# Clustered attention with a Fourier-gated second stage, one core: the order of all engines' work planned anew

## The chip, the cores and the metric

One core of a Trainium2 chip runs the kernel alone. The metric is the time of one execution in device microseconds; the kernel before took 384.34 us in the median of three runs (382.85 to 384.55). The profile is that of one further execution.

## The reference

```python
q_n = q / (norm(q) + 1e-06); k_n = ...; c_n = ...          # q, k, v: (4, 8, 768, 64), 16 centroids a head
q_assign = argmax(einsum('bhsd,hcd->bhsc', q_n, c_n)); k_assign = ...
mask = q_assign[:, :, :, None] == k_assign[:, :, None, :]
scores = where(mask, (q @ k.T) / 8, -1e9)
attn_out = softmax(scores) @ v                              # then heads side by side: x (4, 768, 512)
x1, x2, x3 = split(x @ w_proj, 3)                           # 512 -> 3 * 512
x2_conv = irfft(rfft(x2) * rfft(filter_fft))                # along the 768 positions
out = (x1 * x2_conv * x3) @ w_out
```

The first half is attention in which a query sees only the keys that were assigned to its own centroid. The second half takes the result through three projections, a circular convolution along the sequence (done as products with cosine and sine tables), a gate and an output projection.

## The kernel before, in words

**Attention.** Batches and heads are cut into 8 groups of four heads (`n`), each of two head pairs (`pr`): 16 head pairs. For a group, `routing` transposes q and k on TensorE (L583, L594), copies them out of PSUM (L586, L596, into tile qkP), casts them into the bf16 operands `aug` (L600, the helper's lines 265 for ScalarE and 267 for VectorE and POOL), multiplies with the centroids (L614) and turns the argmax into mask rows, which a DMA adds to the operands (L488). `attention` goes over six key blocks (`sk`) of a pair. For each it forms three score products of 512 columns (helper `product`, L75 as two 64-column halves or L73 as one 128-column product; 288 in all), three exponentials on ScalarE (L697, L700) and eight matmuls with v (L711), which need all three. VectorE sums the exponentials into `acc` (L728 for the first two blocks, in thirds that POOL may also do; L732 for the other four). At a pair's end ScalarE copies the output out of PSUM (L735, osb). The denominators are summed over partitions, either on TensorE (L745, then `total`, L751 and L753, tile den), or for middle groups by accumulating DMAs of POOL (L765), a trip through DRAM (dd, dp) and a small sum on VectorE (`gather`, L775 and L776). Then come a reciprocal (L778), a trip through DRAM that spreads it (dr, then rb by two SP transfers, L782), and one multiplication that gives xT (L811).

**Second stage.** `hyena` runs once a batch (two groups): projections `U` (L845) with copies and sums in tiles tm and uv2 (L854, L859, L864), the spectrum (L466, L872) and its products with the filter (L875, L879, tile y), gate projections `G` (through L75) with copies into x3 (L913, tile x) and products (L916), inverse transforms `I` with copies into od (L939), sums and folds (L941, L951), the gate (L954), and the output projection `W` with copies into ob (L974) and stores (L981). For the first three batches it runs beside the attention of later groups; for the last one it is the kernel's end.

**What sets the order.** `build` makes 1938 pieces. Each has a priority (its due time, in the planner's own clock), the engines that may do it with an assumed duration each, what it reads and writes, and the PSUM bank it opens or frees. `Plan.place` (L114) walks through assumed time: it takes for each engine the pieces that could start, prefers the smallest due time, and so fixes the engine and the place in the engine's queue. `NUDGE` (L41) adds a number to each piece's due time and `ONLY` (L42) fixes the engine of a few hundred pieces. The engines then run their queues strictly in that order, each instruction waiting on semaphores for its inputs. Assumed times are used for nothing else. Banks are handed out by `banks_for` (L223): at most four banks are in use for scores and four for the other work, and a product waits until the bank's earlier reader has ended.

**The shared port.** Pieces marked `lock=True` are SBUF work on VectorE or POOL that the planner keeps from overlapping. In the program, each such POOL piece waits for the last locked VectorE piece placed ahead of it (L1193); VectorE does not wait for POOL. Before the change `gather` has the mark `kind="port"`: it does hold POOL in the program (L1196), but the planner does not know of it.

Of the kernel before, what the change touches and what calls it, by code (L numbers as in the profile page):

```python
# [35 lines left out]
LEAD = 2.99901  # L36
FIRST = 2
BUSY = 8.09741
# [39 lines left out]
class Plan:  # L78
# [6 lines left out]
    def op(self, eng, fn, due, r=(), w=(), alloc=None, free=(), lock=False, byts=0, after=(), kind=None, lat=0.0):  # L85
# [27 lines left out]

    def place(self, free0, banks_for, switch=0.1, wait=0.1, rate=215e3, bonus=10.84378, margin=0.02195, shape=1.63806):  # L114
        free = dict(free0)
        bank_free = [0.0] * 8
        ready = {e: [] for e in free}
        pend = 0
        st = SimpleNamespace(pool=0.0, dve=0.0, bw={}, last=None, kind=None, score=0, o=0, tail=0,
                             held=dict(score=0, fill=0, o=0))  # L120
        st.scores, st.otiles = (sum(o.alloc is not None and o.alloc.cls == c for o in self.ops) for c in ("score", "o"))
        busy = dict.fromkeys(free, 0.0)

        def enqueue(o):
            o.ready = max([d.end - AFTER.get(d.on, 0.0) * (d in o.soft) + (0.06 if o.eng.keys().isdisjoint((d.on,)) or d.byts else 0.0)
                           for d in o.deps] or [0.0])
            if o.kind == "load":
                o.ready = max(o.ready, o.due - LEAD)
            for e in o.eng:
                ready[e].append(o)  # L130

        def take(o):
            if o.alloc is None:
                return
            o.alloc.ids = banks_for(o.alloc, bank_free, st, o)[0]
            for i in o.alloc.ids:
                bank_free[i] = 1e9
            st.score += o.alloc.cls == "score"
            st.o += o.alloc.cls == "o"
            st.held[HOLD.get(o.alloc.cls, "fill")] += o.alloc.n  # L140
            if o.alloc.cls != "o":
                st.tail |= st.o == st.otiles and any(i in (4, 5) for i in o.alloc.ids)

        def done(o, e, t, d, end):
            o.start, o.on = t, e
            o.end = end + AFTER.get(e, 0.0)
            if o.byts:
                s, b = max(o.end + 1.3, st.bw.get(e, 0.0)), o.byts / rate
                for f in [f for f in st.bw if f != e and st.bw[f] > s]:
                    b += min(o.byts / rate, st.bw[f] - s)  # L150
                    st.bw[f] += min(o.byts / rate, st.bw[f] - s)
                st.bw[e] = s + b
                o.end = st.bw[e] + 0.6 + o.lat
            if e == "POOL" and o.lock:
                st.pool = t + d
            if e == "DVE" and o.lock:
                st.dve = t + d
            for h in o.free:
                h.readers -= 1
                h.end = max(h.end, o.end)  # L160
                if not h.readers:
                    st.held[HOLD.get(h.cls, "fill")] -= h.n
# [12 lines left out]
        for o in self.ops:  # L175
            if not o.left:
                enqueue(o)
        while any(ready.values()):
            best = None
            for e, lst in ready.items():  # L180
                f = free[e]
                cand = []
                for o in lst:
                    t = max(f, o.ready)
                    m = margin if e == "PE" else 0.0
                    late = max(f, o.ready + m)
                    if o.alloc is not None:
                        ids = banks_for(o.alloc, bank_free, st, o)
                        if ids is None:
                            continue  # L190
                        t, late = max(t, ids[1]), max(late, ids[1] + m)
                    if o.lock and e in ("POOL", "DVE"):
                        t = late = max(t, st.dve if e == "POOL" else st.pool)
                    cand.append((late, o, t))
                if not cand:
                    continue
                t0 = min(c[0] for c in cand)
                c = min((c for c in cand if c[0] <= t0 + wait + 1e-9), key=lambda c: (
                    c[1].due - (bonus if e == "PE" and st.kind == "pv" == c[1].kind else 0.0)
                    + (shape if e == "PE" and array(c[1], st.last) != st.last else 0.0)  # L200
                    + (BUSY if e == "DVE" and len(c[1].eng) > 1 else 0.0)
                    + (c[0] - t0) * 20, c[1].seq))
# [45 lines left out]
def build(T):  # L248

    P = Plan()  # L250
    op = P.op
# [414 lines left out]
    def attention(n, pr, sins):  # L666
# [88 lines left out]
        if not last:  # L755
            if late:
                op(("SP", .6), lambda e: T.nc.sync.dma_start(T.dd[os][:4, :384], den_()[0:128:32]), te + 2, r=dk,
                   w=[("dd", os)], byts=6e3)
                op(("SP", .6), lambda e: T.nc.sync.dma_start(T.dn, T.dd[os][:4, :384].rearrange("z (a b) -> z a b", b=12)),
                   te + 4, r=[("dd", os)], w=["dn"], byts=6e3)  # L760
            else:
                flat_ = lambda: T.acc[os][:].rearrange("p a b -> p (a b)")
                rows = 64
                while rows >= ROWS:
                    op(("POOL", .8), lambda e, rows=rows: T.nc.gpsimd.dma_start(  # L765
                        flat_()[:rows], flat_()[rows:2 * rows], accum_op=Alu.add), te, r=[], w=AK,
                       byts=rows * 9e3, lat=1.5)
# [348 lines left out]
def kernel(  # L1116
# [70 lines left out]
    for o in order:  # L1187
# [40 lines left out]
```

## Time and profile before

| | |
|---|---|
| median of three runs | 384.34 us (382.85 to 384.55) |
| the profiled execution | 384.85 us, of which the span from first to last instruction is 383.1 |
| TensorE (PE) busy | 364.8 us |
| VectorE (DVE) busy | 347.5 us |
| ScalarE (ACT) busy | 261.6 us |
| POOL busy | 108.6 us |
| first product on TensorE | 4.67 us after the span's start |
| last head pair's last product with v | ends at 336.9 us |
| last matmul | near 378.5 us |

The page counts an engine as busy while an instruction of its own runs; the share of the span says how close it is to being the limit. "Waits" lines give, for an instruction, how long its engine stood idle before it and which instruction or transfer ended that. "The chain that ended last" is followed back from the last instruction, and each engine's share of it says whose work the end waited for. In timeline lines the columns are start in us, duration in us, engine, line, operation, output<-input, form, count, and in brackets the idle time before it with its releaser.

### The profile page before, as it was taken

The numbers are of one execution on the slowest core, as the hardware profiler recorded it, in microseconds if no ns is written. First come the engines' busy times: TensorE is split into PE (matmuls) and PEld (weight loads), VectorE is DVE, ScalarE is ACT, GpSimd is POOL, SyncE is SP. The second block draws the span as 40 slices with busy tenths as digits, with TensorE's granted clock in tenths as the row PEclk, the third lists the DMA queues.
The fourth block names the chain that finished last, engine by engine and source line by source line (L and its number), as shares of the span: only waits on it lengthen the run. The fifth ranks groups of instructions, "written<-read, shape, count | busy, mean of one in ns | idle before, by whom it ended". The sixth has DMA issues, their size and how long they took to land.

```text
span 383.1 us, 8652 instructions
## 1 busy us (share of the span) xinstructions
PE 364.8 (95%) x3323; PEld 208.3 (54%) x3328; DVE 347.5 (91%) x519; ACT 261.6 (68%) x488; POOL 108.6 (28%) x147
## 2 busy tenths in 40 slices
PE   2999998999999999999999999999999999999895
PEld 1564454445445565655555565656554565567682
DVE  8878997999899999989998999989999999899992
ACT  5996979787883978858856569688863747623332
POOL 8432101100022544123432453133320442103600
PEclk9999999999999999999999999999999999999999
DMA  9719965762578587747796876855555642110214
GB/s 221 160 47 220 164 154 135 158 146 63 128 165 157 104 130 151 126 90 122 160 144 147 165 191 134 173 72 89 103 75 132 134 105 37 46 43 2 94 74 164
DMA packets 93861, 47.19 MB, mean 123 GB/s; under 512 B 82088, under 2 KB 87676, under 8 KB 93820
## 3 DMA queue, kind: packets, MB, share of 16 engines
q1 hardware_dynamic: 88620, 37.03, 39.9%
q0 software_dynamic: 2704, 8.98, 17.6%
q10 hardware_dynamic: 2496, 0.62, 0.7%
q8 instruction: 26, 0.43, 0.5%
q14 instruction: 15, 0.12, 0.1%
HBM read 31.59 MB, written 7.40 MB: 102 GB/s over the span
## 4 chain that ended last, share of the span: by engine, by line
PE 55%; DVE 22%; DMA 9%; ACT 7%; issue 5%; SPq 1%; POOL 0%; POOLq 0%; DVEq 0%; ACTq 0%
PE bank L75 22%; PE pair L711 18%; DVE acc L732 5%; DMA rb<-dr 5%; PE bank L845 4%; ACT p L700 3%; DVE tm L875 2%; PE bank L583 2%; PE bank L594 2%; PE bank L614 1%; DVE acc L728 1%; DMA dr<-dn 1%; ACT p L697 1%; DVE xT L811 1%; PE bank L503 1%
## 5 line engine op out<-in xcount | busy, mean ns | idle before, releaser
L711 PE MATMUL pair<-p,vraw 128*64 128x385 f32 x768 | 142.5, 490 | 0.9 <-ACT osb L735 0.6
L700 ACT ACTIVATE p<-bank 128x512 f32<-128x512 f32 x192 | 108.9, 604 | 31.9 <-PE bank L75 26.5
L732 DVE TENSOR_TENSOR acc<-p,acc 128x1536 f32<-128x1536 f32 x64 | 113.0, 1765 | 4.9 <-ACT p L697 2.3
L711 PEld LDWEIGHTS pair<-p,vraw 128*64 128x64 f32 x768 | 53.7, 136 | 49.6 <-issue 42.5
L75 PE MATMUL bank<-aug,aug 80*64 80x512 bf16 (+3 forms) x688 | 75.2, 327 | 2.2 <-DVE den L753 0.5
L697 ACT ACTIVATE p<-bank 128x512 f32<-128x512 f32 x96 | 57.2, 606 | 11.6 <-PE bank L75 10.8
L75 PEld LDWEIGHTS <-aug 128*64 128x64 bf16 (+1 forms) x688 | 40.5, 109 | 38.9 <-issue 28.6
L765 POOL DMA_DIRECT2D acc<-acc x30 | 23.8, 793 | 91.1 <-DMA acc<-acc 42.6
L75 PE MATMUL bank<-xT,wpj 128*64 128x384 bf16 x488 | 44.7, 326 | 0.0
L267 POOL CAST aug<-qkP 64x768 bf16<-64x768 f32 x22 | 20.3, 927 | 71.7 <-DVE acc L732 34.1
L265 ACT COPY qkP<-bank 128x512 f32<-128x512 f32 (+1 forms) x52 | 26.7, 543 | 15.9 <-PE bank L75 8.6
L75 PEld LDWEIGHTS <-wpj 128*64 128x64 bf16 x488 | 29.6, 110 | 13.9 <-issue 3.8
L75 PEld LDWEIGHTS <-y 128*64 128x64 bf16 x512 | 25.5, 110 | 14.4 <-issue 4.4
L728 POOL TENSOR_TENSOR acc<-p,p 128x512 f32<-128x512 f32 x13 | 16.5, 1275 | 53.2 <-ACT p L700 25.7
L875 DVE TENSOR_TENSOR tm<-bank,hm 128x512 f32<-128x512 f32 x44 | 27.9, 681 | 1.0 <-POOL y L879 0.2
L728 DVE TENSOR_TENSOR acc<-p,p 128x512 f32<-128x512 f32 x35 | 24.6, 730 | 2.7 <-ACT p L697 1.7
L265 ACT CAST aug<-qkP 64x768 bf16<-64x768 f32 x29 | 24.0, 831 | 1.6 <-PE bank L75 1.1
L879 POOL TENSOR_TENSOR y<-tm 128x512 bf16<-128x512 f32 x17 | 21.7, 1289 | 10.5 <-DVE tm L875 6.3
L845 PE MATMUL bank<-wpj,xT 128*64 128x512 bf16 x192 | 22.7, 380 | 0.9 <-DVE xT L811 0.9
L75 PE MATMUL bank<-wout,y 128*64 128x512 bf16 x192 | 22.9, 379 | 0.0
L735 ACT COPY osb<-pair 128x770 f32<-128x770 f32 x16 | 12.9, 808 | 9.6 <-PE pair L711 9.5
L811 DVE SCALAR_TENSOR_TENSOR xT<-osb,rb 128x768 bf16<-128x768 f32 x15 | 15.2, 1012 | 3.9 <-DMA rb<-dr 3.9
(161 smaller groups left out, 440.7 us busy)
## 6 DMA issues: line engine op xcount, KB each, us to landing
qkraw<-in_k_dram SPq DMA_DIRECT2D x32, 192.0 KB, 4.6
vraw<-in_v_dram SPq DMA_DIRECT2D x16, 384.0 KB, 4.3
rb<-dr SPq DMA_DIRECT2D x30, 192.0 KB, 3.3
out_dram<-ob SPq DMA_DIRECT2D x11, 512.0 KB, 2.8
qkraw<-in_q_dram SPq DMA_DIRECT2D x29, 192.0 KB, 3.9
acc<-acc POOLq DMA_DIRECT2D x10, 384.0 KB, 4.9
acc<-acc POOLq DMA_DIRECT2D x10, 192.0 KB, 4.1
y<-in_moe_filter_fft_dram SPq DMA_DIRECT2D x4, 384.0 KB, 8.9
```

Of the source, the lines that this page charges most:

```text
L75: T.nc.tensor.matmul(out[64 * i:64 * i + 64], lhsT[:, 64 * i:64 * i + 64], rhs, start=start, stop=stop)
L265: T.nc.scalar.copy(out, in_)
L267: (T.nc.vector if e == "DVE" else T.nc.gpsimd).tensor_copy(out, in_)
L697: T.nc.scalar.activation(o, ap(h).rearrange("p (a b) -> p a b", a=2), Act.Exp, scale=0.125)
L700: T.nc.scalar.activation(flat(s)[:, lo:lo + 512], ap(h), Act.Exp, scale=0.125)
L711: T.nc.tensor.matmul(o[64 * hp:64 * hp + 64, ch, :385], T.vraw[vs][:, hp, sk * D:(sk + 1) * D], T.p[slots[sk]][:, hp, 384 * ch:384 * ch + ...
L728: alu(e).tensor_tensor(o, x, y, op=Alu.add)
L732: T.nc.vector.tensor_tensor(T.acc[os], T.p[slots[sk]][:, :, :S], T.acc[os], op=Alu.add)
L765: op(("POOL", .8), lambda e, rows=rows: T.nc.gpsimd.dma_start(flat_()[:rows], flat_()[rows:2 * rows], accum_op=Alu.add), te, r=[], w=AK, b ...
L845: T.nc.tensor.matmul(ap(h)[64 * i:64 * i + 64], T.xT[xs][:, kt, c:c + 64], T.wpj[:, kt, DM:2 * DM], start=kt == 0, stop=kt == ND - 1)
L875: op(("DVE", .68), lambda e, i=i, cs=cs, r=r, h=h: T.nc.vector.tensor_tensor(T.tm[r][:, cs], ap(h), hmrow(i, (0, 2, 2, 3)[2 * r + cs]), op ...
L879: op({"POOL": 1.5, "DVE": .68}, lambda e, i=i, r=r: alu(e).tensor_tensor(T.y[:, i, r], T.tm[r][:, 0], T.tm[r][:, 1], op=Alu.add if r else ...
```

## The change

Every due-time correction (`NUDGE`, now for all 1938 pieces instead of 1861) and the list of fixed engines (`ONLY`, 233 pieces instead of 227) are new. Four constants that entered the choice are set to zero (`LEAD`, `BUSY`, `bonus`, `shape`), and a piece that could start earlier is preferred less strongly (0.2 instead of 20 for each unit of assumed time). A locked POOL piece is planned to start 0.06 us after the locked VectorE piece instead of at its end, and the latest start that the choice compares keeps its margin. `gather` becomes a locked piece for the planner, and the mark "port" goes. The numbers of the new tables were sought with assumed durations that were scattered at random; the kernel holds only what was found. The pieces themselves, their sizes and their data are the same.

```diff
-LEAD = 2.99901
+LEAD = 0.0
...
-BUSY = 8.09741
+BUSY = 0.0
...
-NUDGE = {0:-51.9627,1:-2.6349,2:38.686,3:-141.578,4:142.779,5:166.407,
...
+NUDGE = {0:-27.3856,1:10.1217,2:73.8109,3:10.6856,4:400.544,5:336.601,
...
-ONLY = {25:"SP",26:"SP",27:"ACT",28:"ACT",29:"SP",30:"SP",53:"ACT",55:"ACT",56:"DVE",
...
+ONLY = {23:"SP",24:"SP",25:"SP",30:"SP",55:"ACT",56:"POOL",59:"ACT",62:"POOL",63:"DVE",
...
-    def place(..., bonus=10.84378, margin=0.02195, shape=1.63806):
+    def place(..., bonus=0.0, margin=0.02195, shape=0.0):
...
                     if o.lock and e in ("POOL", "DVE"):
-                        t = late = max(t, st.dve if e == "POOL" else st.pool)
+                        t = max(t, st.dve + 0.06 if e == "POOL" else st.pool)
+                        late = max(late, t)
...
-                    + (c[0] - t0) * 20, c[1].seq))
+                    + (c[0] - t0) * 0.2, c[1].seq))
...
-                op(("DVE", .68), gather, te + 6, r=["dp"], w=["dn"], kind="port")
+                op(("DVE", .68), gather, te + 6, r=["dp"], w=["dn"], lock=True)
...
-        elif o.on == "DVE" and (o.lock or o.kind == "port"):
+        elif o.lock and o.on == "DVE":
```

What this does to the engines, read from the two programs' instructions: 77 pieces that compute change their engine. Of the casts into `aug` (L600) 35 change among ScalarE, VectorE and POOL; of the first pair sums (L728) three go to POOL and five to VectorE; of the folds (L951) four go to POOL and three to VectorE; three copies into tm (L854), two into x (L913), two into od (L939) go from VectorE to ScalarE; copies of qkP, sim, ob, inv, fw and den go both ways. Each engine keeps nearly the order it had: a piece moves on average by 1.4 places on TensorE, 1.4 on ScalarE, 1.3 on VectorE, 0.7 on POOL and 0.85 on SP. At the start, the loads of the first q and k halves are dealt to SP's and ScalarE's queues in another way, and two more pieces of the angle tables (L359, L362) stand ahead of the centroids' normalisation (L325) on VectorE.

More of the change, by code (lines that the diff above doesn't have):

```diff
@@ new lines @@
+ONLY = {23:"SP",24:"SP",25:"SP",30:"SP",55:"ACT",56:"POOL",59:"ACT",62:"POOL",63:"DVE",75:"ACT",76:"ACT",81:"ACT",83:"DVE",84:"DVE",85:"DVE",87:"ACT",89:"DVE",123:"ACT",125:"DVE",131:"DVE",132:"DVE",134:"DVE",143:"ACT",145:"ACT",149:"ACT",151:"ACT",157:"ACT",161:"ACT",163:"ACT",178:"DVE",179:"DVE",228:"ACT",229:"DVE",235:"POOL",240:"POOL",241:"ACT",246:"POOL",247:"ACT",249:"ACT",250:"DVE",292:"DVE",357:"DVE",358:"POOL",359:"DVE",394:"DVE",404:"ACT",405:"ACT",407:"DVE",409:"DVE",410:"POOL",412:"DVE",416:"ACT",417:"ACT",420:"ACT",462:"POOL",464:"DVE",509:"ACT",514:"ACT",523:"DVE",525:"DVE",526:"DVE",533:"POOL",541:"POOL",549:"DVE",556:"ACT",560:"ACT",563:"DVE",567:"ACT",575:"ACT",578:"POOL",579:"POOL",580:"DVE",582:"ACT",595:"DVE",597:"ACT",601:"ACT",605:"ACT",609:"DVE",610:"DVE",612:"ACT",619:"ACT",624:"ACT",640:"DVE",641:"DVE",690:"ACT",691:"ACT",692:"POOL",693:"ACT",694:"POOL",695:"POOL",697:"DVE",699:"DVE",700:"ACT",701:"ACT",703:"POOL",705:"DVE",747:"DVE",810:"DVE",859:"ACT",860:"ACT",861:"ACT",863:"POOL",864:"ACT",866:"ACT",868:"ACT",871:"DVE",872:"ACT",874:"ACT",916:"POOL",917:"DVE",918:"DVE",965:"DVE",975:"ACT",989:"DVE",990:"POOL",997:"DVE",998:"POOL",1006:"DVE",1008:"ACT",1019:"POOL",1020:"POOL",1021:"DVE",1023:"ACT",1027:"ACT",1035:"DVE",1036:"POOL",1042:"ACT",1046:"ACT",1049:"DVE",1051:"DVE",1053:"DVE",1057:"ACT",1061:"ACT",1064:"DVE",1070:"DVE",1075:"ACT",1078:"ACT",1096:"DVE",1098:"DVE",1146:"ACT",1147:"ACT",1148:"POOL",1150:"ACT",1153:"ACT",1154:"DVE",1156:"ACT",1158:"POOL",1159:"DVE",1162:"ACT",1203:"DVE",1204:"DVE",1205:"DVE",1265:"POOL",1266:"POOL",1314:"ACT",1317:"POOL",1319:"ACT",1322:"ACT",1323:"ACT",1324:"ACT",1326:"POOL",1327:"ACT",1328:"POOL",1330:"ACT",1331:"ACT",1372:"DVE",1373:"DVE",1374:"DVE",1431:"ACT",1435:"DVE",1438:"DVE",1445:"POOL",1446:"POOL",1454:"POOL",1462:"DVE",1464:"ACT",1468:"ACT",1472:"ACT",1475:"POOL",1476:"DVE",1477:"DVE",1483:"ACT",1490:"POOL",1491:"DVE",1492:"DVE",1494:"ACT",1505:"DVE",1506:"DVE",1507:"DVE",1509:"ACT",1517:"ACT",1521:"DVE",1526:"ACT",1529:"ACT",1531:"ACT",1534:"ACT",1536:"ACT",1553:"DVE",1554:"POOL",1601:"ACT",1602:"ACT",1603:"ACT",1604:"ACT",1605:"POOL",1606:"DVE",1607:"ACT",1611:"ACT",1612:"POOL",1613:"ACT",1617:"ACT",1652:"POOL",1713:"DVE",1715:"DVE",1772:"POOL",1809:"ACT",1825:"ACT",1831:"ACT",1837:"DVE",1838:"DVE",1845:"POOL",1853:"POOL",1854:"POOL",1862:"DVE",1869:"ACT",1873:"DVE",1878:"ACT",1886:"ACT",1891:"ACT",1899:"ACT",1904:"ACT",1921:"ACT",1925:"ACT",1932:"ACT"}
@@ L112, in op, with place @@
         return o
-    def place(self, free0, banks_for, switch=0.1, wait=0.1, rate=215e3, bonus=10.84378, margin=0.02195, shape=1.63806):
+    def place(self, free0, banks_for, switch=0.1, wait=0.1, rate=215e3, bonus=0.0, margin=0.02195, shape=0.0):
         free = dict(free0)
```

3 lines of the change are left out of this document (1 added, 2 removed).

## The prediction

> **What bounds the kernel now.** I read the page's busy shares first, then the chain that ended last, then TensorE's and VectorE's own waits, then the timeline around the longest stops of TensorE.
>
> ```profile
> PE 364.8 (95%) x3323; PEld 208.3 (54%) x3328; DVE 347.5 (91%) x519; ACT 261.6 (68%) x488; POOL 108.6 (28%) x147
> ...
> PE 55%; DVE 22%; DMA 9%; ACT 7%; issue 5%; SPq 1%; POOL 0%; POOLq 0%; DVEq 0%; ACTq 0%
> ```
>
> TensorE is busy for 95% of the span and carries over half of the chain; VectorE carries 22% of it. By stretches TensorE is busy for 315.86 of the 321 us from 24 to 345 and VectorE for 298.36. So this is TensorE's kernel, with VectorE close behind: a re-planned order can win only TensorE's stops. The stops are short and named:
>
> ```profile
> 62.04 0.41 PE L75 MATMUL bank<-aug,aug 80*64 80x256 bf16 x4 [0.49 <-DVE hm L446]
> ...
> 62.96 1.28 PE L75 MATMUL bank<-aug,aug 128*64 128x512 bf16 x12 [0.52 <-DVE den L753]
> ```
> ```profile
> 95.46 1.03 PE L73 MATMUL bank<-aug,aug 80*128 80x256 bf16 x5 [0.47 <-ACT p L700]
> ```
> ```profile
> 171.07 1.09 PE L75 MATMUL bank<-aug,aug 80*64 80x256 bf16 x8 [0.26 <-DVE x L916]
> ```
> ```profile
> 207.57 1.70 PE L845 MATMUL bank<-wpj,xT 128*64 128x512 bf16 x14 [0.40 <-DVE xT L811]
> ```
>
> The bracket is TensorE's idle time and what ended it: a score product (L75, L73) waits for a PSUM bank that a VectorE or ScalarE piece has not yet read, or a projection (L845) for its input. The bracket is too small, since ends of matmuls are modelled. From start to start a score takes 0.22 us when nothing waits; from 61.14 to 62.04 one took 0.90, a stop of 0.68. Reckoned so, the stops above 0.11 us between 24 and 345 us sum to 9.2 us; the largest are 41.7 (0.75, the copy of the output pair), 62.0 (0.68), 63.0 (0.71), 95.5 (0.62), 134.0 (0.51), 170.4 to 171.5 (0.91 in three), 207.8 (0.60), 221.7 (0.64) and 292.7 (0.69). This 9.2 is what the change can win in the middle.
>
> **The change part by part.** The profiled execution took 384.85 us, its span 383.1; the median of the runs is 384.34, 0.51 lower. I sum against 384.85 and subtract 0.51 at the end.
>
> *Work on TensorE.* The same 621 pieces stand in nearly the same order: a piece moves 1.4 places on average, 22 at most. Changes of array shape go from 74 to 73 at 0.09 to 0.12 us each. Eighty-five pieces instead of 79 run as one 128-column product instead of two 64-column halves, which costs nothing (128x384 averages 326 ns on L73 and on L75). Sum 0.
>
> *Work on the others.* Net, VectorE loses nine instructions. By the means of their rows: one cast 0.570, one qkP copy 0.644, two sim copies at 0.542, three tm copies at 0.685, two x copies at 0.552, two od copies at 0.553, one fold 0.554, one ob copy 0.686, one fw copy 0.561, less two pair sums at 0.730, one den 0.545 and two inv copies at 0.256: 5.85 us less. ScalarE gains those copies at its prices (tm 0.588, x 0.492, od 0.496, sim 0.479 and so on): 5.2 us more. POOL: one cast more (0.927), one fold more (1.044), two sums less (1.275): 0.6 us less. Summing both orders up to the last accumulation (L732), VectorE has 5.1 us less in front of it; 4.1 are gone by the sixth head pair and the rest stays near 5. None of it is TensorE time, so it counts only where TensorE stops for VectorE.
>
> *The stops, one by one in the new order.* 62.0: its bank was last read by hm (L446), which moves ahead of an accumulation (1.77) and two casts; TensorE then has 2.5 us of work between the bank's two uses: gone, 0.68. 63.0: 1.2 us of cover instead of 0.44: I take 0.5. 95.5: the bank is another, cover 0.23 becomes 0.90, but the score before it now has 0.45 instead of 1.9: gone 0.62, new 0.45. 134.0: bank now freed by an exponential, cover 2.8 instead of 2.2: gone 0.51. 171: the x copy in front goes to ScalarE and the fold to POOL: gone 0.9. 207.8 and 292.7: xT (L811) waits for rb, whose chain starts with the reciprocal on VectorE, and VectorE is 4.6 us lighter by then while TensorE is only 0.9 earlier; but rb's two transfers (3.2 and 4.5 us) are not shortened: half, 0.65. 41.7 stays and loses 0.44 of cover; 221.7 stays (0.22 of cover in both; cover is TensorE's own work, at its usual times, between a bank's last write and its next use). Two smaller ones (53.6, 148.0) get 2.4 and more: gone 0.4. New short covers: a projection of the second batch's gate (0.22 us; I price it at the 0.5 that such stops took) and one of the first batch's (0.65; 0.2). Sum: gone 0.68 + 0.5 + 0.62 + 0.51 + 0.9 + 0.65 + 0.4 = 4.26; new 0.45 + 0.44 + 0.5 + 0.2 = 1.59; net 2.7. Some stops come from no short cover (those behind covers of 2 to 2.5 us sum to 2.5 us), and an order that differs will make some of them elsewhere; I take 0.4 off: **2.3 us less**. From both sides: by cover classes alone (each class's mean stop times its new count) the sum falls by only 0.4; with every VectorE-bound stop gone it falls by about 5.
>
> *The beginning.* The first queries come on one queue instead of two: the second half is issued about 0.3 us later. The centroids' normalisation (L325) now stands behind two more angle pieces (L359 0.61, L362 0.56), so their transposition, at 8.94 now, comes 1.2 us later; behind it on TensorE wait six transposes and the first similarities. Against that, six transposes of 0.21 us move into the idle stretch before it. The similarities start at 11.84 behind ScalarE's copies in any case. Bounds minus 0.3 and plus 1.3; I take 0. A row bears on this: until 13.8 us transposes start 213 ns apart, from 14.7 on 109 ns, though the page shows the clock as granted. Six more transposes at the slower step are in the 1.3.
>
> The Trainium skill, "TensorE: Matmul & The Clock Gate", section "Part 1: The HAM clock gate", says that a TensorE which was idle runs at half rate until one window of about 3.4 us is busy throughout. This trace agrees (from 8.94 on nothing stops it, and 14.55 is fast), and the rule speaks against the new beginning: the busy stretch starts 1.2 us later. By it, as an estimate, the sum would be 0.6 us worse, half of the 1.2 us, which gives 382.6.
>
> *The end.* After the last accumulation VectorE has one x product and one fold more, one od and one tm copy less, one x product later: 0.69 less. TensorE has two gate products fewer there (1.30) and one inverse transform more (0.66). The stop at 361.3 (1.04 idle, on POOL's y) loses and gains the same: 0, bounds 0.7 either way.
>
> *The denominators' sum (L775).* In the program POOL was already held behind it; now the plan knows. It runs ten times at 484 to 493 ns, and the one at 237.47 lay under a POOL fold for all its 489 ns: not stretched. Price 0, at most ten times 0.68 on POOL, which is busy 28%.
>
> *Shared-port stretches.* Beside a POOL sum a VectorE sum took 1384 ns instead of 685; eight such stretches after 24 us cost VectorE 3.3 us. The rule of order is as before; their number can go to none or double, which at the ratio found above (2.3 of 5.85) is 1.3 us either way on TensorE.
>
> *Queues.* No transfer is added. Of SP's 234 pieces 91 change place, by 0.85 places on average and 7 at most (mask rows against loads); an issue takes 0.54 to 1.26 us (L302), so a rb transfer (L782) may start one issue earlier or later: minus 0.6 to plus 0.6 where xT waits for it, 0 taken. POOL's accumulating transfers (L765) shift four times by one piece; they end far ahead of their readers. The rule in the planner that POOL starts 0.06 us after VectorE's locked piece, and the zeroed constants, act through the order alone.
>
> Sum: 384.85 - 2.3 = 382.55, on the median's scale **382.0 us**.
>
> **The rivals.** *Stops only move* (0.25): the plan has been re-dealt, cover classes are alike (20 short covers under 1.1 us in the middle against 27), so the sum falls by 0.4 to 1: 383.4 to 385.3, say 384.0. For it speaks the near-equal order; against it, VectorE's 5 us.
>
> *ScalarE becomes late* (0.20), the slower side. Its work between the last exponentials of successive head pairs grows by 1.8, 2.2, 1.8, 2.2 and 2.7 us in five of them; those exponentials now end 3.1, 2.3, 1.7, 2.5 and 8.7 us before their last product with v starts (timeline). It decides from where growth exceeds lead: three of the five are within 0.5 us of it. If each of the three pays 1 us: 384.3 + 3.0 = 387.3. Against it: L700 waits 26.5 us and L697 10.8 us for TensorE, so ScalarE mostly has nothing to do.
>
> *VectorE's 5 us come through whole* (0.10): where the chain runs through VectorE all the way to the last accumulation: 384.3 - 5.1 = 379.2.
>
> **How the numbers follow.** The forecast has 0.45 and reaches from 380.4 to 383.4. What a measurement can tell from no change is about 0.5%, 1.9 us: 382.4 and 386.3 are the bounds. Faster: two thirds of the forecast's and the last rival: 0.40. Same: the rest of the forecast, the first rival and a little of ScalarE's: 0.41. Slower: 0.19. The range leaves out a tenth at each end: 379.0 to 387.0.
>
> **What would show it.** Right: VectorE's busy time near 342 us and ScalarE's near 267; no idle bracket before the scores around 62, 134 and 171 us; TensorE idle under 4 us from 24 to 345. Wrong: L700's waits for banks on TensorE's side grow around 106, 185 and 234 us (ScalarE); the transposition of the centroids at 10 us followed by 213 ns steps beyond 15 us; new stops of 0.5 us whose releaser is VectorE.

## The result, and the profile after

The changed kernel takes 382.39 us (median of ten runs, 380.94 to 383.36), the kernel before 383.70 us in the same rounds (ten runs, 382.85 to 384.55): ratio 0.9965, interval 0.9948 to 0.9982. That is 1.3 us or 0.35% faster, real but within the 0.5% that had a chance of 0.41, and 0.4 us beside the forecast of 382.0. The profiled executions took 384.85 us before (more than any of those ten) and 381.96 us after. From here on line numbers are the changed kernel's, which are one higher than those of before from L194 on.

The page's busy shares, and the shares of the chain that ended last:

```profile
PE 363.1 (96%) x3303; PEld 208.0 (55%) x3308; DVE 342.1 (90%) x510; ACT 267.3 (70%) x497; POOL 104.8 (28%) x147
...
PE 84%; DVE 8%; ACT 4%; issue 1%; DMA 1%; ACTq 0%; POOL 0%; DVEq 0%; POOLq 0%
```

VectorE and ScalarE stand where the prediction put them (342 and 267), and the chain now runs through TensorE for 84% instead of 55%. TensorE's timeline at the places that were shown of before (62 to 63, 95, 171, 208 us):

```profile
62.64 0.84 PE L75 MATMUL bank<-aug,aug 80*64 80x512 bf16 x8
63.65 1.09 PE L75 MATMUL bank<-aug,aug 80*64 80x512 bf16 x10 [0.17 <-DVE qkP L268]
```
```profile
95.38 1.25 PE L73 MATMUL bank<-aug,aug 80*128 80x512 bf16 x6 [0.46 <-ACT p L701]
```
```profile
169.33 1.48 PE L75 MATMUL bank<-aug,aug 128*64 128x512 bf16 x16
170.64 1.46 PE L712 MATMUL pair<-p,vraw 128*64 128x385 f32 x8
```
```profile
205.66 3.62 PE L846 MATMUL bank<-wpj,xT 128*64 128x512 bf16 x32
```

The brackets at 62 (hm), 171 (x) and 208 (xT) are gone; one short one is left at 63.65, and the one at 95 has come back, one score earlier in the order. So the middle is better. The beginning is not. TensorE's first rows, before and then after:

```profile
4.67 1.51 PE L594 MATMUL bank<-ident,qkraw 128*128 128x128 f32 x6 [4.67 <-DMA qkraw<-in_q_dram]
8.94 0.42 PE L333 MATMUL bank<-ident,sd 128*64 128x128 f32 x1 [2.75 <-DVE sd L330]
9.15 2.77 PE L594 MATMUL bank<-ident,qkraw 128*128 128x128 f32 x12
11.84 2.77 PE L503 MATMUL bank<-qkP,cbd 128*32 128x384 f32 x8
```
```profile
6.07 2.79 PE L595 MATMUL bank<-ident,qkraw 128*128 128x128 f32 x12 [6.07 <-DMA qkraw<-in_q_dram]
11.45 0.42 PE L334 MATMUL bank<-ident,sd 128*64 128x128 f32 x1 [2.59 <-DVE sd L331]
11.67 1.49 PE L595 MATMUL bank<-ident,qkraw 128*128 128x128 f32 x6
13.09 2.77 PE L504 MATMUL bank<-qkP,cbd 128*32 128x384 f32 x8
```

The first matmul starts 1.4 us later, the centroids' transposition (L334) 2.5, the similarities (L504) 1.25, and the first score product at 22.95 us instead of 21.48.

For all kernels below the stops of TensorE are reckoned in the same way as in the prediction (start to start, above 0.11 us). "Rest" is the time from the first score to the end of the last computing instruction. The last three columns stand for one profiled execution each, the ratio for all runs; the kernel before took 383.6 to 384.1 us in the other rounds, so kernels of different rounds are compared by the ratio. The eight traces that begin as before (before, e3, e5, e8 to e12) have the first score at 20.6 to 21.5 us, 21.1 on average, the five that begin as changed (changed, e7, e1, e4, e6) at 22.6 to 23.2, 22.8 on average.

| kernel | median us | ratio to before (95%) | first score at | stops from there to 345 us | rest |
|---|---|---|---|---|---|
| before | 383.70 | | 21.48 | 9.90 | 358.0 |
| changed | 382.39 | 0.9965 (0.9948 to 0.9982) | 22.95 | 5.22 | 353.7 |
| e7: changed again | 382.97 | 0.9971 (0.9956 to 0.9986) | 22.56 | 5.76 | 354.8 |
| e1: changed, loads as before | 382.91 | 0.9986 (0.9965 to 1.0006) | 22.56 | 7.21 | 356.2 |
| e2: changed, normalisation early | 383.82 | 0.9998 (0.9978 to 1.0018) | 23.34 | 6.67 | 355.6 |
| e3: changed, beginning as before | 381.24 | 0.9921 (0.9895 to 0.9947) | 21.15 | 6.64 | 355.5 |
| e10: e3 with the changed loads | 380.87 | 0.9935 (0.9911 to 0.9959) | 21.00 | 5.66 | 354.0 |
| e11: e10 with wout's load later | 381.10 | 0.9940 (0.9922 to 0.9957) | 20.86 | 5.77 | 354.1 |
| e4: before, changed beginning | 386.87 | 1.0074 (1.0053 to 1.0095) | 23.16 | 9.07 | 357.7 |
| e5: before, VectorE lighter | 383.44 | 0.9983 (0.9971 to 0.9995) | 20.57 | 9.14 | 357.5 |
| e8: before, one cluster | 383.16 | 0.9985 (0.9972 to 0.9998) | 21.43 | 8.64 | 357.2 |
| e6: changed, VectorE heavier | 385.08 | 1.0024 (1.0003 to 1.0045) | 22.96 | 6.55 | 356.3 |
| e9: e3 with 49 moves | 380.88 | 0.9922 (0.9898 to 0.9947) | 20.95 | 10.39 | 357.7 |
| e12: e9, fewer transfer waits | 380.57 | 0.9930 (0.9910 to 0.9951) | 21.47 | 6.81 | 354.2 |

The theory under test: **the gain is the stops that the new order takes from the middle, and the beginning gives about half of it back.** Rivals: the gain comes from VectorE's lighter load and not from the order; the beginning's delay is taken up by a later wait; the difference is scatter. In every experiment the kernel holds its plan as a written list of the 1938 pieces with engine and bank, so that a piece can be moved with nothing else changing; the diffs are of that list.

### The profile page after: what moved, and what is told of

Same layout as the page of the kernel before. It is cut to its first block, busy times and chain, and to the rows that moved or that the text cites. A ratio compares the mean times of both kernels' runs of the same rounds, so it can differ in the third digit from the quotient of the medians.

```text
span 380.2 us, 8604 instructions
## 1 busy us (share of the span) xinstructions
PE 363.1 (96%) x3303; PEld 208.0 (55%) x3308; DVE 342.1 (90%) x510; ACT 267.3 (70%) x497; POOL 104.8 (28%) x147
## 3 DMA queue, kind: packets, MB, share of 16 engines
q0 software_dynamic: 2704, 8.98, 16.7%
## 4 chain that ended last, share of the span: by engine, by line
PE 84%; DVE 8%; ACT 4%; issue 1%; DMA 1%; ACTq 0%; POOL 0%; DVEq 0%; POOLq 0%
PE pair L712 32%; PE bank L75 32%; PE bank L584 4%; PE bank L846 4%; PE bank L73 3%; PE bank L615 3%; ACT p L701 2%; PE bank L628 1%; PE bank L595 1%; ACT p L698 1%; PE bank L746 1%; DMA rb<-dr 1%; DVE tm L876 1%; PE bank L504 1%; ACT aug L266 1%
## 5 line engine op out<-in xcount | busy, mean ns | idle before, releaser
L701 ACT ACTIVATE p<-bank 128x512 f32<-128x512 f32 x192 | 108.3, 609 | 26.5 <-PE bank L75 21.8
L712 PEld LDWEIGHTS pair<-p,vraw 128*64 128x64 f32 x768 | 53.6, 136 | 49.0 <-issue 40.9
L75 PE MATMUL bank<-aug,aug 80*64 80x256 bf16 (+3 forms) x680 | 73.8, 327 | 0.6 <-ACT p L701 0.5
L698 ACT ACTIVATE p<-bank 128x512 f32<-128x512 f32 x96 | 57.3, 607 | 7.8 <-PE bank L75 7.4
L75 PEld LDWEIGHTS <-aug 128*64 128x64 bf16 (+1 forms) x680 | 39.3, 109 | 37.5 <-issue 25.2
L766 POOL DMA_DIRECT2D acc<-acc x30 | 23.8, 792 | 111.5 <-DVE acc L733 63.9
L75 PE MATMUL bank<-xT,wpj 128*64 128x384 bf16 x472 | 43.6, 326 | 0.7 <-ACT p L698 0.5
L266 ACT COPY qkP<-bank 128x512 f32<-128x512 f32 (+1 forms) x53 | 27.3, 543 | 15.0 <-PE bank L75 9.0
L75 PEld LDWEIGHTS <-wpj 128*64 128x64 bf16 x472 | 28.7, 110 | 13.7 <-issue 4.5
L880 POOL TENSOR_TENSOR y<-tm 128x512 bf16<-128x512 f32 x17 | 21.5, 1277 | 15.4 <-DVE tm L876 5.4
L266 ACT CAST aug<-qkP 64x768 bf16<-64x768 f32 x29 | 24.0, 830 | 1.3 <-PE bank L75 0.6
L729 POOL TENSOR_TENSOR acc<-p,p 128x512 f32<-128x512 f32 x11 | 14.2, 1292 | 19.8 <-DVE acc L729 7.8
L584 PEld LDWEIGHTS bank<-ident,qkraw 128*128 128x128 f32 x144 | 15.6, 141 | 5.4 <-issue 3.1
L584 PE MATMUL bank<-ident,qkraw 128*128 128x128 f32 x144 | 18.4, 277 | 0.0
```

The source lines that it names most:

```text
L75: T.nc.tensor.matmul(out[64 * i:64 * i + 64], lhsT[:, 64 * i:64 * i + 64], rhs, start=start, stop=stop)
L266: T.nc.scalar.copy(out, in_)
L584: T.nc.tensor.transpose(bank(h.ids[i // 4])[:, ts(i % 4, 128)], raw(ss[i // NT], i % NT), T.ident[:, ::-1] if 3 <= i < NT else T.ident)
L698: T.nc.scalar.activation(o, ap(h).rearrange("p (a b) -> p a b", a=2), Act.Exp, scale=0.125)
L701: T.nc.scalar.activation(flat(s)[:, lo:lo + 512], ap(h), Act.Exp, scale=0.125)
L712: T.nc.tensor.matmul(o[64 * hp:64 * hp + 64, ch, :385], T.vraw[vs][:, hp, sk * D:(sk + 1) * D], T.p[slots[sk]][:, hp, 384 * ch:384 * ch + ...
```

## The experiments

**e1, the first loads.**

```diff
 # first loads of q and k (L303); q1, k1 the first pair's two halves, q2, k2 the second's
-SP: q1a q1b k1a q2b k2b    ACT: q2a k1b k2a
+SP: q1a k1a k1b k2a k2b    ACT: q1b q2a q2b
```

> The changed kernel with one thing put back: the first pair's loads are dealt to the two queues as before (the two halves of the first q on SP and ACT, both halves of k behind them on SP), 381.0 to 382.4 us against the changed kernel's 382.4. In the changed kernel the first matmul starts at 6.07 us instead of 4.67, and the first score at 22.95 instead of 21.48. Theory A (the beginning's 1.5 us come from the loads): the first matmul is back at about 4.7, the first score at about 21.5, and the time falls by about 1.4 us to 381.0. Theory B (they come from the centroids' normalisation, whose L326 waits behind two more pieces of the angles and starts at 9.65 instead of 7.66): the first matmul is back at 4.7, but the centroids' transposition stays near 11.4, the first score near 22.9, and the time stays at 382.4 within 0.3. Theory C (what the beginning costs is taken up by a later wait): the first score is earlier and the time the same.

Measured: 382.91 us, no gain. TensorE's first rows:

```profile
5.16 1.51 PE L595 MATMUL bank<-ident,qkraw 128*128 128x128 f32 x6 [5.16 <-DMA qkraw<-in_q_dram]
7.32 1.51 PE L595 MATMUL bank<-ident,qkraw 128*128 128x128 f32 x6 [0.65 <-DMA qkraw<-in_k_dram]
11.45 0.42 PE L334 MATMUL bank<-ident,sd 128*64 128x128 f32 x1 [2.61 <-DVE sd L331]
```

The transposes come 0.9 us earlier and TensorE then waits for the same normalised centroids until the same 11.45. The first score is at 22.56, as in e7, which has the changed loads. Theory A falls. Theory B holds for these rows; the time is 0.5 us above its 382.4, outside the 0.3 that it allowed, and the stops behind the beginning were 7.21 us in this execution instead of 5.22.

**e2, the normalisation alone.**

```diff
 # VectorE, pieces by line
-356 1007 358 360 356 358 360 363 363 [326-331] 360 [339-340]
+356 1007 [326-331] 358 360 356 358 [339-340] 360 363 363 360
```

> The changed kernel with one thing moved: on VectorE the centroids' normalisation (the six instructions at L326 to L331) goes ahead of seven pieces of the angles, right behind the first product at L360 can be started, and the two copies at L339 and L340 go ahead of four of them; loads, TensorE, ScalarE and POOL keep their order. Theory B (the beginning is bound by the normalisation): the transposition at L334 comes near 9 us instead of 11.45, the similarities near 11.5 instead of 13.1, the first score about 1.2 to 1.5 us earlier, and the time falls to about 381.1. Theory A (loads): the transposition is earlier, but the similarities wait for the evictions of the late q and k, the first score is within 0.3 of 22.95 and the time is 382.4. Theory C (taken up later): first score earlier, time the same.

Measured: 383.82 us, slower than the changed kernel, and none of the three theories as they were put:

```profile
8.77 0.42 PE L334 MATMUL bank<-ident,sd 128*64 128x128 f32 x1
8.98 1.02 PE L595 MATMUL bank<-ident,qkraw 128*128 128x128 f32 x6
9.93 0.83 PE L504 MATMUL bank<-qkP,cbd 128*32 128x384 f32 x2
13.51 2.77 PE L504 MATMUL bank<-qkP,cbd 128*32 128x384 f32 x6 [2.75 <-ACT qkP L266]
16.21 0.87 PE L595 MATMUL bank<-ident,qkraw 128*128 128x128 f32 x6
```

The transposition comes at 8.77 as B wants, but the third similarity product waits until 13.51 for ScalarE's copies of qkP (L266). ScalarE's timeline shows why:

```profile
10.43 0.52 ACT L366 ACTIVATE fw<-tm 128x384 bf16<-128x384 f32 x1 [1.38 <-DVE tm L360]
10.86 0.46 ACT L266 COPY qkP<-bank 128x384 f32<-128x384 f32 x1
...
12.50 0.60 ACT L368 ACTIVATE fw<-ob,half_pi 128x384 bf16<-128x384 f32 x1
13.00 0.83 ACT L266 COPY qkP<-bank 128x384 f32<-128x384 f32 x2
```

The copies stand behind sines of the angle tables, and those wait for the pieces that were put back on VectorE. So the beginning is one chain over three engines: VectorE's angle pieces feed ScalarE's sines, ScalarE's copies stand behind the sines, and VectorE's normalisation stands behind the angle pieces. Moving the normalisation alone only moves the wait.

**e3 and e4, the whole beginning.** All 125 pieces ahead of the first score are exchanged between the two plans, banks renamed to fit.

> The changed kernel from its first score on, with everything ahead of it (the 125 pieces up to there: loads, angles, normalisation, transposes, their engines and order) as before; PSUM banks renamed so that both fit. Theories A and B alike: first matmul near 4.7, first score near 21.5, and the time falls by about 1.4 us to 381.0, since the stops of the middle (9.4 us before, 5.2 us in the changed kernel) stay as they are in the changed kernel. Theory C (the beginning's loss is taken up by a later wait, and the kernels differ by 1.3 us for the middle alone): the first score is 1.4 us earlier and the time stays at 382.4 within 0.4.

> The kernel before from its first score on, with everything ahead of it as in the changed kernel. Theories A and B alike: first matmul near 6.1, first score near 23.0, and the time rises by about 1.4 us to 385.1 (383.7 for the kernel before in these rounds). Theory C (taken up later): 383.7 within 0.4. If the middle is worth the whole 4.2 us of stops that are gone, this kernel stands 2.7 to 4.2 us above the changed one.

Measured: 381.24 and 386.87 us. Against the kernel before in their rounds (383.89) that is 2.65 less and 2.98 more; the changed kernel is 1.3 less. So the old beginning is worth 1.3 us on the new middle, as forecast, and the new beginning costs the old middle 3.0 instead of 1.4. Of the 3.0, the trace shows 1.7 until the first score (23.16 against 21.48) and 0.8 more in two stops right behind the joint (0.65 at 24.7 us and 0.30 at 25.8, of which before has 0.18); the changed kernel's trace has no such stops there, so they are put down to joining the two. The other 0.5 isn't found. "Taken up later" falls on both sides.

**e10, the loads once more, on the good beginning.** e3 with the changed kernel's dealing of the first loads (the lines of e1's diff, the other way round).

> The kernel that begins as before and goes on as changed, but with the first loads dealt to the queues as in the changed kernel (both halves of the first q on SP). Theory A (the beginning's cost lies in the loads): first matmul near 6, and the time rises by 1 us or more to 382.4. Theory B (it lies in what stands ahead of the centroids' normalisation and of the first evictions on VectorE and ScalarE): the first matmul comes later, the similarities still start near 11.9, and the time stays at 381.2 within 0.5.

Measured: 380.87 us. The first matmul comes 0.6 us later than in e3 (5.11), and the rest does not notice:

```profile
5.71 1.51 PE L595 MATMUL bank<-ident,qkraw 128*128 128x128 f32 x6 [5.71 <-DMA qkraw<-in_q_dram]
8.93 0.42 PE L334 MATMUL bank<-ident,sd 128*64 128x128 f32 x1 [1.71 <-DVE sd L331]
9.14 2.77 PE L595 MATMUL bank<-ident,qkraw 128*128 128x128 f32 x12
11.84 2.30 PE L504 MATMUL bank<-qkP,cbd 128*32 128x384 f32 x8
```

The loads cost nothing that can be measured; the beginning's price lies in the rest of what e3 exchanges, the order and the engines of its pieces.

**e5 and e6, load against order.** Thirteen PSUM copies (L620, L855, L914, L940, L975) change sides, with no other change.

```diff
 # e5, plan of before           # e6, changed plan
-sim tm x ob od x13: DVE       -sim tm x ob od x13: ACT
+sim tm x ob od x13: ACT       +sim tm x ob od x13: DVE
```

> The kernel before with thirteen PSUM copies given from VectorE to ScalarE as in the changed kernel (three of sim at L620, three of tm at L855, two of x at L914, two of ob at L940, three of od at L975), every order and bank as before: VectorE is lighter by some 7.5 us, TensorE's order untouched. Theory L (the changed kernel gains because VectorE is lighter): the stops that wait for VectorE (62.0, 63.0, 134.0, 171: 2.8 us) shrink, and the time falls by 1.5 to 2.5 us to about 381.8. Theory O (the stops went because single pieces and banks were put elsewhere, the load itself is worth little): 383.8 within 0.6. Theory S (ScalarE gets late): above 384.8, with new stops of TensorE in front of scores and products with v that wait for ScalarE's exponentials.

> The changed kernel with the same thirteen copies given back from ScalarE to VectorE, order and banks as changed; VectorE's busy time rises from 342 to about 349.5. Theory L: the gain of the middle (2.9 to 4.2 us of stops) goes and the time rises by 2.5 us or more to 385 to 387. Theory O: the stops at 62.0, 63.0, 134 and 171 stay away, new ones of at most 0.5 us appear only right behind the thirteen, and the time rises by less than 1 us to 382.4 to 383.3.

Measured: e5 383.44 us against 384.05 (0.6 less), e6 385.08 against 382.97 of e7 in the same rounds (2.1 more). In e5 VectorE is busy for 342.0 us, as in the changed kernel, and yet the two stops at 62 and 63 (here 61 and 62) are what they were, 0.68 and 0.71:

```profile
61.13 0.41 PE L75 MATMUL bank<-aug,aug 80*64 80x256 bf16 x4 [0.49 <-DVE hm L447]
62.05 1.50 PE L75 MATMUL bank<-aug,aug 128*64 128x512 bf16 x16 [0.51 <-DVE den L754]
```

The one at 171 shrinks from 0.91 to 0.21, because x itself was among the thirteen. In e6 VectorE is back at 347.5 us, and the old stops stay away: the middle's sum rises by 0.8 to 6.55, the stops behind 345 us by 0.6, the first score came 0.4 later. By the times, e5 lies where theory O put it and e6 where theory L did, so neither theory holds alone. Lighter VectorE in the old order: 0.6. New order (with the rest of its engine changes) and the heavy VectorE: 1.0 slower than before, which with a beginning that costs 1.2 to 1.9 (by the ratios of e3 and e10 against those of the changed kernel) is a middle better by 0.2 to 0.9. Both together: 1.1 faster, a middle better by 2.3 to 3.0. The new order was made for these engines, and each half is worth little without the other.

**e7, the changed kernel again.**

> The changed kernel itself, on the same chip and in the same rounds as the three others, for a second measurement of its stops: 382.4 us, ratio 0.9965. Stops of TensorE that come from the order return to within 0.1 us at the same pieces (41.7: 0.69, 95.4: 0.61, 219.4: 0.64, 256: 0.64); those that are chance of one execution (waits for transfers: the products at 126 and 207.8) come or go.

Measured: 382.97 us. Three of the four stops of the order return as forecast: 0.69, 0.61, 0.64 at 43.0, 95.6, 219.9 us; the gate product at 256 has 0.44 instead of 0.64. The ratio, 0.9971 (0.9956 to 0.9986), leaves 1 out once more: the gain is not scatter. New in this execution are 0.65 at 81.9 (denominators behind acc, L746) and 0.20 at 127.

**e8, one cluster of stops.**

```diff
 # VectorE, plan of before, around 60 us
-acc cast cast reciprocal hm cast den qkP
+acc hm cast cast reciprocal den qkP cast
```

> The kernel before with three moves on VectorE alone around 62 us: hm (L447) right behind the accumulation that ends at 60.1, ahead of two casts; the denominators' copy (L750) and the copy of the transposes (L587) ahead of a third cast. The stop at 62.0 (0.68) loses its cause. Additive theory: both stops, 62.0 and 63.0, go, and the time falls by 1.2 to 1.4 us to 382.5. Chain theory: the stop at 63.0 waits for the accumulation, the denominators' products and their copy behind one another, which are not shortened, so it grows by what is taken away in front of it (0.71 to about 0.9), only the follower at 64.2 goes, and the time falls by 0.2 to 0.5 us to 383.4.

Measured: 383.16 us against 384.05, 0.9 less, with an interval of 0.1 to 1.1. In the trace the chain theory holds: the stop at 62.0 is gone, and the next one has grown from 0.71 to 0.91.

```profile
61.09 0.63 PE L75 MATMUL bank<-aug,aug 80*64 80x512 bf16 x6
62.46 1.55 PE L75 MATMUL bank<-aug,aug 128*64 128x512 bf16 x16 [0.74 <-DVE den L754]
```

So 0.48 of 1.39 us comes through. What the runs show beyond that is within their interval, which leaves out the additive theory's 1.2 to 1.4.

**e9, e11 and e12, towards a version that beats both.** e9 is e3 with 49 more pieces moved:

```diff
 # TensorE, two of 32 moves, at 131 and 61 us
-L467, gate product, score       -transposes, denominators, score, score
+L467, score, gate product       +transposes, score, score, denominators
 # SP, the one move
-oh->ohT, load of v
+load of v, oh->ohT
```

> The kernel that begins as before and goes on as changed, with 49 further pieces moved by a few places each (32 of TensorE, 8 of ScalarE, 8 of VectorE, and one load of v on SP ahead of the mask's transposing transfer instead of behind it), so that something else stands between a bank's last write and its next use at the stops that came back in every run (41.6, 61.9, 94.2, 130.9, 219.3, 256 and the tail). Replayed with the durations of that kernel's own trace, the moves take 3.0 us of its stops. Theory A (time is work plus stops, and what is taken from a stop comes through): 381.2 less 3.0, 378.2 us, ratio to the kernel before near 0.985. Theory M (a stop taken away shows up at the next wait, since VectorE and ScalarE are nearly as busy): 379.8 to 381.2. Stops above 0.11 us between the first score and 345 us: under 4.5 us by A, above 5.5 by M.

Measured: 380.88 us, and A falls. The stops at 61.9, 130.9, 219.3 us and 349 us did go or shrank to 0.2; the profiled execution (384.32 us, the longest of its six; the others took 380.2 to 382.5) has others instead:

```profile
103.31 0.85 PE L628 MATMUL bank<-ident,sim 128*128 128x128 f32 x6 [1.15 <-DVE sim L268]
...
129.28 1.01 PE L73 MATMUL bank<-aug,aug 80*128 80x512 bf16 x3 [2.47 <-DMA aug<-ohT]
```

Both have a transfer behind them. VectorE stood 2.17 us at 97 us for rb (L812, ahead of the copy of sim in its queue), and the copies of ohT (L489) on SP started 9.25 us behind the transposing transfer (L658). The waits of SP's queue between 110 and 126 us, before, after and in e9:

```profile
SPq L488 <- DMA ohT<-oh: 0.9, 1, 0.9
```
```profile
SPq L489 <- DMA ohT<-oh: 3.4, 1, 3.4
```
```profile
SPq L489 <- DMA ohT<-oh: 7.5, 1, 7.5
```

In the changed plan POOL issues the load of wout (L1052) at 111.1 us, ahead of the transposing transfer (114.5), since the pair sum that stood between moved to VectorE; before, it was issued at 115.7, behind it (114.3). e11 and e12 put it back:

```diff
 # POOL, by line
-766 1052 766 766 766
+766 766 766 766 1052
 # VectorE (e12 only): xT (L812) three to five pieces later, at 72, 97 and 244 us
```

> The kernel with the old beginning and the changed loads (380.87 us, ten runs of it between 380.1 and 383.9), with one instruction moved: POOL issues the load of wout (L1052, 512 KB, first read near 201 us) behind its fourth accumulating transfer, near 127 us, instead of behind the first, at 109.2. Before, it was issued 1.4 us behind the mask's transposing transfer (L658), which then let the next issue go after 2.9 us; in the changed order it goes 3.4 us ahead of it, and the issue behind that transfer waits 5.4 to 9.2 us, so that the score at 125 us stood 0 to 2.4 us. Theory W (the load of wout holds the transposing transfer up): the copies of ohT start within 3.5 us of L658, the score at 125 does not stop in the profile, the time falls by 0.2 to 0.6 us to about 380.5 and no run is above 382.5. Rival V (the load of v, issued right behind L658, or the accumulating transfers do it): 5 us and more as before, time and spread the same.

> The kernel with 49 pieces moved (380.88 us), with the load of wout at the same later place and with three of VectorE's xT pieces (L812, at 72, 97 and 244 us, which stand first in VectorE's queue and wait up to 2.2 us for the transfer of rb) put behind three to five pieces that do not need it; xT is read 12 us later or more. Theory A (stops taken away come through once the waits for transfers are gone): the stops at 82, 103, 129 and 133 us (0.67, 1.19, 2.42, 1.21 in that kernel's profile) go, the stops from the first score to 345 us sum to under 4.5 us, and the time is 378.3 to 379.3. Theory M (each stop taken away shows up at the next wait): 380 to 381, and the sum of stops stays above 5.5 us.

Measured: 381.10 and 380.57 us. In e11 SP's wait is 3.1 us and the copies start 5.1 us behind L658, where W wanted 3.5 and e10 had 6.4. Since the same order without this move shows 5.4 to 7.2, the load of wout isn't shown to be the cause, though e11 and e12 (5.0) have the two shortest delays of the changed order; the second accumulating transfer (L766) also goes out 1.6 us earlier than before relative to L658, and that was not tried. No stop stands at 125 us and no run is above 381.9 (e10: 383.9), on six runs against nine. In e12 xT no longer waits (0.3 us), but the next piece in VectorE's queue does:

```profile
DVE dn L779 <- DMA dn<-dd: 3.0, 1, 3.0
```

and the transposes of sim at 103 us stop for 1.06 us as in e9. The sum of stops, 6.81, is M's. The 51 and more moves of e9 and e12 are worth nothing that can be measured beside e3 and e10. All five with the old beginning lie between 380.6 and 381.2 us, 2.5 to 3.2 us under the kernel before in their rounds and 1.2 to 1.8 under the changed one; e10 is the simplest of them that has the changed loads, e3 the one that differs least from both parents.

## Why the prediction was right, point by point

- *What bounds the kernel.* Right. Rest less stops (and less the stops behind 345 us, 1.43 and 1.64) is 346.7 us before and 346.8 after: the work of TensorE is unchanged, as the sum of 0 said. From 24 to 345 us TensorE is idle for 2.9 us (busy for 318.12 of 321), under the 4 that were to show the forecast right.
- *Work on the others.* VectorE 5.4 us less (forecast 5.85), ScalarE 5.7 more (5.2). POOL 3.8 less (0.6); what its pieces do to VectorE stands under the beginning.
- *The stops, one by one.* 62.0, 134.0, 171, 53.6 and 148.0 are gone as forecast. 63.0 has become 0.34. 95.5 came back at the score before it, at 0.61 instead of 0.45. 221.7 stays at 0.64 exactly. The new ones at the gate projections are 0.44 to 0.64 (0.5) and 0.39 (0.2). 41.7 stays at 0.69; the 0.44 that I added for its lost cover did not come. 207.8 and 292.7 are gone in every trace of the new order, 1.29 instead of 0.65; in the old order they scatter from execution to execution (0.37 to 0.90 and 0 to 0.71 in e4, e5 and e8), because VectorE waits there for rb. The net term of 2.3 was too small: from the first score to 345 us, 9.2 us on average of before, e5 and e8, and 6.1 of the seven traces with the changed order and engines (the changed kernel, e7, e1, e2, e3, e10, e11), are 3.1; the changed kernel's own two traces alone (5.22 and 5.76) would make it 3.7.
- *The beginning.* **This step failed.** I took 0 with a bound of +1.3, on the ground that the similarities wait for ScalarE's copies in any case. In neither profile do they: from the centroids' transposition on (8.94 before, 11.45 after) TensorE works without a break until the similarities (11.84 and 13.09), and ScalarE's copies ahead of them had ended at 11.59 and 12.12. (In e2, where the transposition is early, they do wait for copies.) So a late transposition comes through, less the six transposes that moved in front of it: 2.5 less 1.3 is the 1.25 that the similarities came later. And the transposition came 2.5 us later, not 1.2. The two angle pieces cost their 1.2. A further 0.57 is there before VectorE's first angle product: L1013 takes 1.39 us instead of 0.55 while POOL clears `aug`, which now comes ahead of `inv` in POOL's queue. And 0.52 is L328, which takes 0.68 us instead of 0.16 while POOL casts `aug`; the last 0.2 is spread over other pieces. The rows before, then after:

```profile
1.99 0.55 DVE L1012 TENSOR_SCALAR s0t<-s0t 64x3 f32<-64x3 f32 x2
8.05 0.16 DVE L327 TENSOR_TENSOR s<-s,s 128x1 f32<-128x1 f32 x1
10.75 0.84 ACT L265 COPY qkP<-bank 128x384 f32<-128x384 f32 x2
```
```profile
1.92 1.44 POOL L1031 MEMSET aug<- 64x768 bf16 x2
1.99 1.39 DVE L1013 TENSOR_SCALAR s0t<-s0t 64x3 f32<-64x3 f32 x2
9.88 0.82 POOL L268 CAST aug<-qkP 64x768 bf16<-64x768 f32 x1 [0.80 <-DVE s L326]
10.04 0.68 DVE L328 TENSOR_TENSOR s<-s,s 128x1 f32<-128x1 f32 x1
11.29 0.83 ACT L266 COPY qkP<-bank 128x384 f32<-128x384 f32 x2
```

The five traces that begin as changed have these same stretched durations within 0.01 us, the eight that begin as before have the short ones, and in e2, where no cast runs beside it, L328 takes 0.16. No run moves POOL's pieces alone, so their share of the price is read from the rows and not tested. In all the beginning cost 1.5 us in the two profiles, 1.7 by the averages of the first score, and 1.2 to 1.9 by the ratios of e3 and e10. The loads, which I priced at 0.3, cost nothing that can be measured (e10). One sign of being wrong did come: the late transposition with 213 ns steps beyond 15 us.

- *The half rate.* The profile's page shows the clock as granted from the start, yet transposes start 213 ns apart until 16.7 us after the change (14.6 before) and 109 ns apart from there. The estimate by the Trainium skill, "TensorE: Matmul & The Clock Gate", section "Part 1: The HAM clock gate", gave half of the delay, 0.6 us. The measured delay is more than twice that; the estimate was worked out from a transposition 1.2 us late, and it was 2.5 late.
- *The end*: right within its bounds (stops behind 345 us 1.43 before, 1.64 after). *The denominators' sum* (L776): right as far as the rows go, it runs ten times at 481 to 494 ns as it did before (484 to 493); no run takes its hold on POOL away.
- *Queues.* I counted the shifts of L766, and not that the load of wout behind it passes the transposing transfer. It is 512 KB on a queue whose transfers run beside those of SP. In the changed kernel's two profiles the score behind it loses 0 and 0.20 us, in e2 and e6 0, in e10 0.38, in e1, e3 and e9 1.07, 1.09 and 2.42; a range of 0.6 was too small for that. That the load of wout is the cause isn't shown (e11).
- *The rivals.* "Stops only move" is wrong for the sum, and right for single stops taken out by hand (e8, e9, e12). "ScalarE becomes late": TensorE's waits for exponentials (L698, L701) are 0.5 to 0.7 us a row, as before. "VectorE's 5 us whole": the relief alone is worth 0.6 (e5).

So 382.0 came out near 382.4 with the middle 0.8 better than forecast, the beginning 1.5 and the end 0.2 worse, and the scale 0.6 better: the profiled execution stood 1.15 above the median of the later runs, where I had subtracted 0.51. That it came so near is in part luck: the beginning's miss of 1.5 was made up for by a middle and a scale that were each better than I had them. With the middle and the end as measured but the beginning at 0, the same sum would have given 380.8, which is where the kernels with the old beginning lie (380.6 to 381.2).

## What to carry to other kernels

Where one engine is 95% busy and a second 90%, take stops from several executions: those that return at the same piece to the hundredth belong to the order, those that come and go have a transfer at the head of an in-order queue behind them, and moving the waiting piece only shows the next transfer. A beginning is a chain over several engines; test it by exchanging all of it, since single moves (e1, e2) gain nothing even where the whole is worth more than 1 us. And a lighter second engine is worth its time only in an order that was made for it.

## What the runs showed of the hardware that was not expected

**How long the half rate lasts is scatter of its own.** From the last long idle time on TensorE works without a break, and the step of transposes goes from 213 to 109 ns after 5.6 us (before), 5.25 (changed), 3.4 (e7, the same program as the changed kernel), 3.5 (e1, e5), 5.0 (e3), and not within 5.6 us in e4; the other traces but e2 lie between these. The steps can be read from rows of six transposes. These are the six behind the similarities, in e7 and in the changed kernel:

```profile
15.32 0.88 PE L595 MATMUL bank<-ident,qkraw 128*128 128x128 f32 x6
```
```profile
15.79 1.29 PE L595 MATMUL bank<-ident,qkraw 128*128 128x128 f32 x6
```

At the full rate they take 0.88 us; in 1.29 the rate changes after the fourth. That alone moves the first score by 0.4 us between two executions of one program. The Trainium skill, "TensorE: Matmul & The Clock Gate", section "Part 1: The HAM clock gate", has a window of about 3.4 us that runs freely; if one whole window must be busy, that gives 3.4 to 6.8 us as an estimate, and the runs above agree. In e2 the full rate came at 9.4 us, was lost in an idle time of 2.75 us, and came back 2.7 us after it: both shorter than that window, so with such a window it need be neither idle nor busy throughout.

**A transposing transfer takes longer beside others.** The copies behind L658 started 2.9 to 3.8 us after it in the old order (before, e4, e8, e5), and 5.0 to 9.25 us after it in the changed one, where POOL's transfers (0.4 and 0.5 MB) are under way. The Trainium skill, "DMA: Bandwidth & Descriptors", section "Queues, rings and completion order", says that an engine takes packets from its queues in turn; by that a short transfer would share with a long one. That fits; e11 did not show which of POOL's two transfers it is.
